# A convolution, layer norm and feed-forward kernel on one core: all 2,576 places of its order of operations replaced

## The chip, the core and the metric

The kernel runs on one core of a Trainium2 chip. The metric is the time of one execution on the device in microseconds (us). The median of several executions is compared; a separate execution is profiled, and every duration below comes from it.

A core has five engines, each with a queue of its own that it works off strictly in order: PE (TensorE: matrix products; PEld is its weight load), DVE (VectorE), ACT (ScalarE), POOL (GpSimd) and SP (SyncE, which here issues transfers and computes nothing). Transfers ("DMA") run beside the engines. An engine goes past an instruction only when what that instruction waits for has happened, so everything behind a waiting instruction on the same engine waits too.

## The reference

```python
# x (8, 4224, 192), weight_gen (8, 4224, 8 heads, 7 taps)
w = softmax(weight_gen, axis=-1)
y[b, s, h, :] = sum(w[b, s, h, k] * x_padded[b, s + k, h, :] for k in range(7))   # 24 wide a head
xn = (y - mean(y)) / sqrt(var(y) + 1e-6) * g_ln
out = y + relu(xn @ w_ch1) @ w_ch2          # 192 -> 768 -> 192
```

## The kernel before

The 33,792 tokens lie as 128 partitions x 264 columns, and the work goes by **groups** of four columns: group 0, 4, 8, ... 260, 66 in all (group 108 is columns 108 to 111). A group passes five steps.

1. SP loads x (`load`) and the taps (`wload`). DVE, POOL and ACT make the softmax, for twelve columns at a time (`max`, `sub`, `exp`, `sum`, `rcp`, `inv`, `mul`).
2. The convolution: DVE multiplies x by the taps in four instructions a group (`c0` to `c3` on line 527, three of them 1,536 wide into buffers `pr`, one 768 wide into `y`). Two of the six partial sums are added by accumulating transfers that POOL issues (`d0`, `d1`, line 533), four by POOL itself (`a0` to `a3`, line 530). The first four chunks go another way, over PE (`z`, line 548).
3. The layer norm: ACT makes the sums and the scaled rows (`sums`, `squares`, `rstd`, `xh` on line 631, `hi` on line 651), DVE five small steps (`newton`), POOL the low half of a split into two 16-bit halves (`lo`, line 664). SP turns the group by a transposing transfer (`turn`, line 668) into `xT`. There are two buffers `xh`, three `xT`.
4. The first product on PE: three `unit`s of 36 matmuls a group (line 686), each into one of two PSUM buffers `ph`. ACT evicts a unit with a relu (`relu`, line 701, into `hh`), DVE what its rounding left (`hlo`, line 703). Both must be done before PE may write that `ph` again, two units later.
5. The second product: two halves of 72 matmuls (`p0` and `p1`, line 737), for the group before the one whose units they stand among. Between them stands an empty instruction on SP (`hop`, line 747): `p0` must have ended before `hop`, and `hop` before `p1`. It costs nothing itself, but it stands in SP's queue behind transfers. DVE adds the result to `y` (`f`, line 789) and SP stores it (`u`, line 797).

Program order is made by a planner that records every operation with the engine that it runs on and what it needs. The order is not worked out in the kernel: `PLACE` gives each of the 2,576 operations a number, by kind and in the order in which that kind is recorded, and `order()` sorts by it. Each engine's queue is that sorted list cut down to its own operations. Where a pool has several buffers, the one whose last user has the lowest place is taken, so places also choose buffers.

Transposes and accumulating transfers are kept apart: a `turn` waits for the landing of the last `d0` or `d1` placed ahead of it, and the other way round.

```python
    def order(self):
        out = sorted(self.ops, key=lambda o: o.place)
...
                    b.slot = min(range(len(tenant[b.pool])), key=lambda i: freed(tenant[b.pool][i]))
...
            if o.kind in last:
                o.behind, last[o.kind] = last["turn" if o.kind == "add" else "add"], o
```

Of the kernel before, what the change touches and what calls it, by code (L numbers as in the profile page):

```python
# [32 lines left out]
        'wload': (1, 4, 28, 42, 57, 90, 73, 168, 448, 452, 507, 743, 618, 896, 787, 1151, 1181, 1307, 1553,  # L33
        1634, 1517, 1896, 1902),
        'load': (5, 14, 17, 32, 35, 75, 83, 109, 188, 121, 76, 182, 260, 236, 273, 363, 303, 497, 513, 390,
# [3 lines left out]
        'w_load': (39, 56, 53, 43, 44, 69),  # L39
        'w_load2': (115, 142),  # L40
        'w_as': (58, 61),
        'w_av': (62, 64, 71),
        'w_an': (92,),
        'w_cs': (66, 70),
        'w_cv': (77, 78, 81),
        'w_cn': (93,),
        'w_s1': (97, 98, 104, 108, 122),
        'w_h': (123, 135, 140, 146),
        'w_l': (153, 151),
        'w_m': (172, 180, 169, 165),  # L50
        'w_c2s': (124, 129, 155, 157),
        'w_c2v': (130, 133, 138, 158, 160, 161),
        'w_c2n': (152, 173),
        'w_s2': (177, 181, 184, 186, 198, 200, 211, 220),
        'max': (2, 7, 31, 55, 67, 117, 134, 258, 522, 464, 698, 858, 652, 1083, 1148, 1337, 1399, 1499, 1568,
        1730, 1612, 1962, 1996),
        'sub': (3, 8, 46, 72, 120, 250, 359, 439, 536, 672, 755, 987, 884, 1110, 1205, 1358, 1452, 1565, 1649,
        1766, 1943, 2020, 2100),
        'exp': (6, 12, 47, 84, 126, 256, 377, 465, 568, 750, 788, 996, 893, 1160, 1294, 1361, 1518, 1650,
        1653, 1831, 1994, 2099, 2112),  # L60
        'sum': (9, 15, 48, 99, 131, 268, 398, 469, 573, 771, 792, 998, 1049, 1172, 1299, 1365, 1519, 1679,
        1669, 1854, 2007, 2140, 2131),
        'rcp': (10, 24, 50, 102, 208, 342, 423, 524, 667, 807, 928, 1022, 1147, 1204, 1312, 1371, 1611, 1693,
        1677, 1919, 2027, 2164, 2205),
        'inv': (11, 26, 54, 118, 235, 356, 445, 528, 668, 859, 946, 1023, 1168, 1267, 1386, 1486, 1641, 1694,
        1792, 1961, 2072, 2189, 2238),
        'mul': (13, 30, 59, 189, 298, 399, 521, 637, 745, 863, 965, 1085, 1193, 1304, 1416, 1520, 1642, 1744,
        1870, 1983, 2086, 2190, 2343),
        'keep': (18, 34),
# [20 lines left out]
        'copy': (60, 74, 110, 167),  # L90
        'sums': (68, 82, 127, 125, 178, 174, 215, 213, 249, 253, 280, 275, 314, 323, 349, 351, 394, 434, 418,
# [7 lines left out]
        'squares': (80, 85, 147, 136, 190, 179, 226, 241, 271, 262, 291, 282, 338, 337, 355, 354, 395, 435,  # L99
# [7 lines left out]
        'rstd': (86, 149, 191, 242, 294, 361, 436, 511, 598, 671, 738, 815, 878, 959, 1036, 1111, 1186, 1248,  # L107
        1325, 1424, 1485, 1555, 1624, 1732, 1793, 1866, 1938, 2014, 2084, 2168, 2227, 2304, 2385, 2437, 2500),
        'newton': (87, 150, 194, 243, 297, 362, 437, 512, 599, 673, 740, 816, 880, 969, 1047, 1114, 1195,
# [912 lines left out]
```

## Time and profile before

| | us |
|---|---|
| median of 3 runs | 868.94 |
| lowest and highest | 864.72, 872.02 |
| profiled execution, its own time | 867.45 |
| its span, first to last instruction | 865.4 |
| PE busy in the span | 826.8 |
| DVE busy in the span | 771.2 |

The profiled execution took 1.49 us less than the median. Its span is 2.05 us shorter than its own time. Busy times of one engine are unions: two instructions that overlap count once. A matmul is shown longer than the distance to the next, because they are pipelined.

### The profile page before, as it was taken

What the parts mean: (1) busy time and instruction counts of PE and PEld (TensorE: products, weight loads), DVE (VectorE), ACT (ScalarE), POOL (GpSimd) and SP (SyncE); (2) the same over time, 40 slices, a digit from 0 to 9 for tenths busy, and PEclk for the clock granted to TensorE, in tenths of its full rate; (3) what the DMA queues carried; (4) which work ended last, traced back from release to release, by engine and by line L of the source; (5) the groups of instructions that cost most, each with busy time, mean ns of one, the idle gap of its engine ahead of it and who ended that gap; (6) DMA issues with size and microseconds to landing.
All of it is one profiled execution on the core that took longest, in us unless ns stands there. A gap on an engine that the chain in (4) does not pass through costs nothing.

```text
span 865.4 us, 37738 instructions
## 1 busy us (share of the span) xinstructions
PE 826.8 (96%) x16691; PEld 799.8 (92%) x16691; DVE 771.2 (89%) x863; ACT 683.5 (79%) x1797; POOL 728.9 (84%) x489
## 2 busy tenths in 40 slices
PE   5968999999999999999999899999999999999998
PEld 5547999999999999998999899999999999999987
DVE  6999999999999999999999799999999998775433
ACT  3888888978898798898789787979788888679721
POOL 6999899999999998999989888999999888777100
PEclk9979999999999999999999999999999999999999
DMA  8687778899969988879969776887886766644253
GB/s 223 157 203 148 156 150 169 179 190 202 194 149 188 198 187 185 164 143 216 198 137 176 194 169 143 190 170 182 175 186 148 155 152 148 120 103 92 68 112 93
DMA packets 146411, 140.91 MB, mean 163 GB/s; under 512 B 108487, under 2 KB 110415, under 8 KB 146247
## 3 DMA queue, kind: packets, MB, share of 16 engines
q1 hardware_dynamic: 127799, 88.95, 43.9%
q0 software_dynamic: 18144, 49.55, 30.7%
q8 instruction: 130, 2.13, 1.0%
q14 instruction: 34, 0.28, 0.1%
q10 hardware_dynamic: 304, 0.00, 0.0%
HBM read 36.43 MB, written 25.95 MB: 72 GB/s over the span
## 4 chain that ended last, share of the span: by engine, by line
PE 36%; DVE 13%; ACT 4%; POOL 4%; issue 3%; SPq 1%; DMA 1%; DVEq 0%; POOLq 0%; ACTq 0%
PE ph L686 18%; PE po L737 17%; DVE pr L527 5%; DVE hlo L703 3%; POOL y L530 3%; DVE y L527 1%; ACT hh L701 1%; DVE y L789 1%; ACT junk L585 1%; PE ph L766 1%; ACT xh L631 1%; DMA pr<-pr 1%; POOL hl L664 1%; ACT junk L580 1%; SPq L668 0%
## 5 line engine op out<-in xcount | busy, mean ns | idle before, releaser
L530 POOL TENSOR_TENSOR y<-y,pr 128x768 f32<-128x768 f32 x252 | 499.9, 2063 | 22.3 <-DVE pr L527 9.4
L686 PE MATMUL ph<-xT,c_w 64*128 64x256 f16 x7128 | 419.5, 272 | 9.0 <-DVE hlo L703 6.2
L686 PEld LDWEIGHTS <-c_w 64*128 64x128 f16 x7128 | 380.5, 95 | 23.1 <-issue 9.7
L737 PE MATMUL po<-c_w2h,hh 64*128 64x192 f16 x3120 | 387.2, 243 | 4.3 <-SPq L747 3.9
L737 PE MATMUL po<-c_w2l,hh 64*128 64x192 f16 x3120 | 387.1, 243 | 2.4 <-issue 2.4
L737 PE MATMUL po<-c_w2h,hlo 64*128 64x192 f16 x3120 | 387.1, 243 | 0.0
L527 DVE TENSOR_TENSOR pr<-x,wn 128x1536 f32<-128x1536 f32 (+1 forms) x193 | 332.2, 1736 | 2.8 <-DMA x<-in_x_dram 1.6
L737 PEld LDWEIGHTS <-hh 64*128 64x128 f16 x6240 | 303.7, 94 | 8.9 <-SPq L747 5.1
L703 DVE SCALAR_TENSOR_TENSOR hlo<-ph,hh 128x1024 f16<-128x1024 f32 x198 | 239.5, 1217 | 57.1 <-ACT hh L701 56.6
L701 ACT ACTIVATE hh<-ph 128x1024 f16<-128x1024 f32 x198 | 199.7, 1012 | 104.5 <-PE ph L686 103.8
L737 PEld LDWEIGHTS <-hlo 64*128 64x128 f16 x3120 | 172.2, 94 | 0.0
L664 POOL TENSOR_TENSOR hl<-xh,hl 128x768 f16<-128x768 f32 x66 | 123.2, 1931 | 36.2 <-ACT hl L651 36.2
L533 POOL DMA_DIRECT2D pr<-pr x126 | 123.6, 1135 | 27.3 <-DVE pr L527 14.9
L631 ACT ACTIVATE xh<-y,s 128x192 f32<-128x192 f32 x264 | 124.6, 535 | 16.9 <-DVE s L619 14.5
L585 ACT ACTIVATE junk<-y,s 128x192 f32<-128x192 f32 x264 | 119.5, 453 | 6.7
L580 ACT ACTIVATE junk<-y 128x192 f32<-128x192 f32 x264 | 94.8, 359 | 15.4 <-POOL y L530 9.8
L789 DVE SCALAR_TENSOR_TENSOR y<-po,c_fs,y 128x768 f32<-128x768 f32 (+1 forms) x66 | 65.8, 997 | 7.2 <-PE po L737 7.1
L527 DVE TENSOR_TENSOR y<-x,wn 128x768 f32<-128x768 f32 (+1 forms) x67 | 62.1, 933 | 1.1 <-ACT e L487 1.0
L651 ACT ACTIVATE hl<-xh 128x768 f16<-128x768 f32 x66 | 55.0, 837 | 1.0
L580 ACT ACTIVATION_READ_ACCUMULATOR junk<-y 128x1 f32 x264 | 49.6, 188 | 0.0
L585 ACT ACTIVATION_READ_ACCUMULATOR junk<-y,s 128x1 f32 x264 | 49.4, 187 | 0.0
L548 PE MATMUL ph<-pr,ident 128*128 128x192 f32 (+1 forms) x96 | 27.8, 447 | 12.4 <-DVE pr L527 10.4
(75 smaller groups left out, 324.4 us busy)
## 6 DMA issues: line engine op xcount, KB each, us to landing
pr<-pr POOLq DMA_DIRECT2D x126, 384.0 KB, 5.6
x<-in_x_dram SPq DMA_DIRECT2D x65, 384.0 KB, 5.5
out_dram<-y SPq DMA_DIRECT2D x64, 384.0 KB, 4.2
w<-in_weight_gen_dram SPq DMA_DIRECT2D x21, 336.0 KB, 5.6
pr<-in_moe_w_ch_dram SPq DMA_DIRECT2D x2, 576.0 KB, 5.6
xT<-hl SPq DMA_TRANSPOSE x66, 3.4
hh<-in_moe_w_ch_dram SPq DMA_DIRECT2D x1, 768.0 KB, 10.3
out_dram<-y SPq DMA_DIRECT2D x4, 192.0 KB, 2.6
```

Source lines behind the costliest of these rows:

```text
L527: E.tensor_tensor(out=ov, in0=xv, in1=wv, op=ALU.mult)
L530: Q.tensor_tensor(out=flat(0), in0=flat(0), in1=flat(k), op=ALU.add)
L533: return Q.dma_start(flat(to), flat(k), accum_op=ALU.add, max_dma_last_dim=CHUNK * D * 4)
L580: A.activation(junk, at(y)[:, j, :], AF.Identity, scale=-1.0 / D, accum_out=at(s4)[:, 3, t : t + 1])
L585: A.activation(junk, at(y)[:, j, :], AF.Square, bias=at(s4)[:, 3, t : t + 1], accum_out=at(s4)[:, 0, t : t + 1])
L631: A.activation(paired(xh, t), at(y)[:, i, :].rearrange("p (c q) -> p c q", q=P // 2), AF.Identity, bias=at(s4)[:, 3, g + t : g + t + 1], s ...
L664: lambda xh=xh, hl=hl: Q.tensor_tensor(out=halves(hl, True), in0=pairs(xh), in1=halves(hl, False), op=ALU.subtract),
L686: T_.matmul(ph[:, r, v * 2 * P : (v + 1) * 2 * P], W["w1"][rows, WB[r][c], w, f : f + P], xv[rows, a, c, :, :], start=(v == 0 and k == 0), ...
L701: lambda: A.activation(at(hh)[:, us, :], at(ph), AF.Relu), [ph], [(hh, u)])
L703: lambda: V.scalar_tensor_tensor(out=at(hlo)[:, us, :], in0=at(ph), scalar=0.0, in1=at(hh)[:, us, :], op0=ALU.max, op1=ALU.subtract),
L737: made.append(T_.matmul(at(po)[:, z, e * D : (e + 1) * D], token(b, 2 * z + e, j)[rows], W[w][rows, j, :], start=(ph == 0 and e == 0 and k ...
L789: V.scalar_tensor_tensor(out=ysl, in0=at(po)[:, zs[0] : zs[-1] + 1, : 2 * D], scalar=W["fs"][:, 0:1], in1=ysl, op0=ALU.mult, op1=ALU.add)
```

## The change

`PLACE` is the one thing that changes: every list in it has new numbers. The operations, their buffers' sizes and counts and all other code stay. The author's words for it: the same operations and buffers; all 2,576 places come from a new search whose replays hold late instruction blocks and long transfer issues.

PE's own order keeps 346 of 351 operations where they were; the five others are convolution sums in the first 16 operations. Of the others, 552 of 669 DVE operations, 688 of 775 of ACT, 397 of 482 of POOL and 236 of 299 of SP stand at another number of their queue, by 2 to 4 positions on the mean and 37 at most.

The last lines of the lists of `turn` and of `hop` (the last numbers are those of the last groups: for `turn` 252, 256, 260; for `hop` 248, 252, 256, 260):

```diff
-        'turn': (148, 195, 251, 285, 336, 370, 411, 432, 489, 505, 554, 581, 631, 654, 718, 727, 797, 804,
...
-        2137, 2181, 2223, 2254, 2285, 2298, 2353, 2330, 2405, 2448, 2476, 2507, 2517, 2520),
...
-        'hop': (240, 286, 324, 372, 405, 460, 493, 515, 559, 596, 626, 664, 719, 762, 801, 829, 871, 894, 949,
...
-        2278, 2301, 2324, 2359, 2391, 2426, 2461, 2484, 2515, 2531, 2546, 2560),
...
+        'turn': (157, 197, 255, 290, 336, 364, 404, 415, 494, 522, 557, 583, 633, 664, 721, 732, 788, 802,
...
+        2151, 2140, 2216, 2253, 2285, 2300, 2363, 2392, 2429, 2444, 2486, 2510, 2511, 2537),
...
+        'hop': (261, 291, 333, 380, 403, 444, 474, 528, 566, 602, 639, 679, 722, 753, 794, 840, 877, 919, 952,
...
+        2260, 2309, 2342, 2370, 2414, 2455, 2473, 2497, 2514, 2527, 2546, 2564),
```

In the rows of the order below a number behind a name is the buffer's. An empty instruction such as `hop` has no row.

**POOL while the pipeline fills, up to the low half of group 8** (L664 into hl_89; L533 are accumulating transfers, L530 adds, L458 the `sub` of a softmax, L953 a step of the weights). Before:

```order
39 L533 DMA pr_84<-pr_84 128x768
40 L533 DMA pr_82<-pr_82 128x768
41 L533 DMA pr_86<-pr_86 128x768
42 L533 DMA pr_81<-pr_81 128x768
43 L530 TENSOR_TENSOR y_73<-y_73,pr_80 128x768
44 L530 TENSOR_TENSOR y_72<-y_72,pr_84 128x768
45 L953 TENSOR_TENSOR c_w2l<-hlo_97,c_w2h 128x1152
46 L533 DMA pr_85<-pr_85 128x768
47 L533 DMA pr_83<-pr_83 128x768
48 L530 TENSOR_TENSOR y_72<-y_72,pr_86 128x768
49 L664 TENSOR_TENSOR hl_89<-xh_87,hl_89 128x2x384
50 L458 TENSOR_TENSOR e_104<-w_64,mx_99 128x672
```

After:

```order
39 L533 DMA pr_84<-pr_84 128x768
40 L530 TENSOR_TENSOR y_73<-y_73,pr_80 128x768
41 L533 DMA pr_81<-pr_81 128x768
42 L533 DMA pr_86<-pr_86 128x768
43 L533 DMA pr_85<-pr_85 128x768
44 L533 DMA pr_83<-pr_83 128x768
45 L533 DMA pr_82<-pr_82 128x768
46 L530 TENSOR_TENSOR y_72<-y_72,pr_84 128x768
47 L953 TENSOR_TENSOR c_w2l<-hlo_97,c_w2h 128x1152
48 L458 TENSOR_TENSOR e_104<-w_66,mx_99 128x672
49 L530 TENSOR_TENSOR y_72<-y_72,pr_86 128x768
50 L664 TENSOR_TENSOR hl_89<-xh_87,hl_89 128x2x384
```

Six transfers that stood as four and two stand as one and five, and one `sub` more stands ahead of the low half. On SP, not shown, `turn` of group 8 has moved from behind `hop` of group 4 (places 251 and 240) to ahead of it (255 and 261).

**ACT around the relu of the first unit of group 216** (L701, the row into hh_94 from ph_111 behind L631 or L430; L631 scales rows of groups 224 and 228 into xh, L585 and L580 are sums). Before:

```order
717 L701 ACTIVATE hh_95<-ph_112 128x1024
718 L580 ACTIVATE junk_109,s_107<-y_68 128x192 x2
719 L585 ACTIVATE junk_109,s_107<-y_68,s_107 128x192 x2
720 L631 ACTIVATE xh_87<-y_67,s_106 128x3x64 x2
721 L631 ACTIVATE xh_88<-y_75,s_106 128x3x64 x4
722 L701 ACTIVATE hh_94<-ph_111 128x1024
723 L631 ACTIVATE xh_87<-y_67,s_106 128x3x64 x2
```

After:

```order
714 L701 ACTIVATE hh_95<-ph_112 128x1024
715 L585 ACTIVATE junk_109,s_106<-y_71,s_106 128x192 x4
716 L608 ACTIVATE s_106<-s_106,bias 128x8
717 L609 ACTIVATE s_106<-s_106 128x8
718 L610 ACTIVATE s_106<-s_106 128x8
719 L430 COPY x<-x 128x1152
720 L701 ACTIVATE hh_94<-ph_111 128x1024
721 L631 ACTIVATE xh_88<-y_71,s_106 128x3x64 x2
722 L631 ACTIVATE xh_87<-y_74,s_106 128x3x64 x4
```

The scaled rows, which need a free buffer `xh`, have moved from ahead of the relu to behind it.

**SP near the end** (L668 are `turn`s, the last three those of groups 252, 256 and 260; L797 are stores). Before:

```order
198 L668 DMA_TRANSPOSE xT_91<-hl_90 128x12x128
199 L797 DMA out_dram<-y_67 16x8x768
200 L668 DMA_TRANSPOSE xT_93<-hl_89 128x12x128
201 L797 DMA out_dram<-y_68 16x8x768
202 L668 DMA_TRANSPOSE xT_92<-hl_90 128x12x128
203 L797 DMA out_dram<-y_70 16x8x768
```

After:

```order
201 L668 DMA_TRANSPOSE xT_91<-hl_90 128x12x128
202 L668 DMA_TRANSPOSE xT_93<-hl_89 128x12x128
203 L797 DMA out_dram<-y_77 16x8x768
204 L797 DMA out_dram<-y_76 16x8x768
205 L668 DMA_TRANSPOSE xT_92<-hl_90 128x12x128
```

By the numbers in the diff, `hop` of group 252 stood behind all three turns (2531 against 2507, 2517 and 2520); now it stands behind two of them (2527 against 2510 and 2511) and ahead of that of group 260 (2537).

## Rows read from the trace of the kernel before

**Rows 1.** The page's part 1: busy us (share of the span), instructions.

```profile
PE 826.8 (96%) x16691; PEld 799.8 (92%) x16691; DVE 771.2 (89%) x863; ACT 683.5 (79%) x1797; POOL 728.9 (84%) x489
```

**Rows 2.** Busy time by stage: PE, PEld, DVE, ACT, POOL; granted clock, DMA share, GB/s.

```profile
0.00:53.90 53.90, 35.24 (x131) 24.96 (x131) 45.16 (x75) 33.50 (x90) 45.64 (x34) 0.92 0.78 197
53.90:95.10 41.20, 34.74 (x615) 30.28 (x616) 39.20 (x52) 36.10 (x102) 40.20 (x30) 0.90 0.72 153
95.00:385.00 290.00, 288.91 (x6113) 285.06 (x6110) 285.07 (x307) 251.05 (x672) 275.49 (x185) 1.00 0.85 178
```

**Rows 3.** Groups by line: count | busy us, mean ns of one | idle before, releasers.

```profile
L686 PE MATMUL ph<-xT,c_w 64*128 64x256 f16 x7128 | 419.5, 272 | 9.0 <-DVE hlo L703 6.2 <-DMA xT<-hl 1.9
L527 DVE TENSOR_TENSOR pr<-x,wn 128x1536 f32<-128x1536 f32 x191 | 330.3, 1745 | 1.2
L703 DVE SCALAR_TENSOR_TENSOR hlo<-ph,hh 128x1024 f16<-128x1024 f32 x198 | 239.5, 1217 | 57.1 <-ACT hh L701 56.6
```

**Rows 4.** PE's waits from 95 us on: total, times, longest.

```profile
PE po L737 <- SPq L747: 3.9, 3, 1.6
PE po L737 <- issue: 2.4, 1, 2.4
PE ph L686 <- DVE hlo L703: 1.9, 3, 1.3
```

**Rows 5.** DVE's waits from 95 to 385 us, the longest of three rows.

```profile
DVE hlo L703 <- ACT hh L701: 0.5, 2, 0.3
```

**Rows 6.** Timeline of POOL: first of the six adds, group 8's low half, the next two.

```profile
59.58 0.87 POOL L533 DMA_DIRECT2D pr<-pr  x1
...
72.39 1.80 POOL L664 TENSOR_TENSOR hl<-xh,hl 128x768 f16<-128x768 f32 x1
74.00 1.51 POOL L458 TENSOR_TENSOR e<-w,mx 128x672 f32<-128x672 f32 x1
75.32 1.94 POOL L530 TENSOR_TENSOR y<-y,pr 128x768 f32<-128x768 f32 x1
```

**Rows 7.** SP and PE then: first hop (of 65), group 8's turn, its units.

```profile
L747 SPq EVENT_SEMAPHORE  x65: 17/17/17, 76.4 to 850.2; - x65
...
76.59 1.40 SPq L668 DMA_TRANSPOSE xT<-hl  x1
...
81.58 5.77 PE L686 MATMUL ph<-xT,c_w 64*128 64x256 f16 x72 [1.94 <-DMA xT<-hl]
```

**Rows 8.** ACT, DVE and PE around the first unit of group 216.

```profile
713.99 1.86 ACT L631 ACTIVATE xh<-y,s 128x192 f32<-128x192 f32 x4 [2.27 <-POOL hl L664]
715.76 1.00 ACT L701 ACTIVATE hh<-ph 128x1024 f16<-128x1024 f32 x1
...
716.79 1.22 DVE L703 SCALAR_TENSOR_TENSOR hlo<-ph,hh 128x1024 f16<-128x1024 f32 x1 [1.79 <-ACT hh L701]
...
718.07 0.48 PE L686 MATMUL ph<-xT,c_w 64*128 64x256 f16 x5 [1.35 <-DVE hlo L703]
```

**Rows 9.** SP and PE at the hop of group 252.

```profile
824.75 2.81 SPq L668 DMA_TRANSPOSE xT<-hl  x1
827.61 0.59 SPq L797 DMA_DIRECT2D out_dram<-y  x1
...
828.31 0.26 PE L737 MATMUL po<-c_w2h,hh 64*128 64x192 f16 x2 [1.58 <-SPq L747]
```

**Rows 10.** SP's turn ahead of the hop of group 108.

```profile
389.20 2.26 SPq L668 DMA_TRANSPOSE xT<-hl  x1
```

**Rows 11.** PE at 481 us, and the busy times and clock from 480 to 485.

```profile
481.43 0.26 PE L737 MATMUL po<-c_w2l,hh 64*128 64x192 f16 x2 [2.43 <-issue]
...
480.00:485.00 5.00, 3.57 (x42) 3.22 (x43) 3.31 (x4) 2.96 (x9) 4.84 (x4) 0.71 0.35 67
```

**Rows 12.** The page's part 3: queue of the accumulating transfers, and that of instructions.

```profile
q0 software_dynamic: 18144, 49.55, 30.7%
q8 instruction: 130, 2.13, 1.0%
```

More of the change, by code (lines that the diff above doesn't have):

```diff
@@ L32 @@
 PLACE = {
-        'wload': (1, 4, 28, 42, 57, 90, 73, 168, 448, 452, 507, 743, 618, 896, 787, 1151, 1181, 1307, 1553,
-        1634, 1517, 1896, 1902),
-        'load': (5, 14, 17, 32, 35, 75, 83, 109, 188, 121, 76, 182, 260, 236, 273, 363, 303, 497, 513, 390,
[3 rows of a table removed]
[L39 to L69, printed above, removed]
[20 rows of a table removed]
-        'copy': (60, 74, 110, 167),
-        'sums': (68, 82, 127, 125, 178, 174, 215, 213, 249, 253, 280, 275, 314, 323, 349, 351, 394, 434, 418,
[7 rows of a table removed]
-        'squares': (80, 85, 147, 136, 190, 179, 226, 241, 271, 262, 291, 282, 338, 337, 355, 354, 395, 435,
[7 rows of a table removed]
-        'rstd': (86, 149, 191, 242, 294, 361, 436, 511, 598, 671, 738, 815, 878, 959, 1036, 1111, 1186, 1248,
@@ L108 @@
-        1325, 1424, 1485, 1555, 1624, 1732, 1793, 1866, 1938, 2014, 2084, 2168, 2227, 2304, 2385, 2437, 2500),
-        'newton': (87, 150, 194, 243, 297, 362, 437, 512, 599, 673, 740, 816, 880, 969, 1047, 1114, 1195,
[14 rows of a table removed]
-        'wake': (154,),
[4 rows of a table removed]
-        'turn': (148, 195, 251, 285, 336, 370, 411, 432, 489, 505, 554, 581, 631, 654, 718, 727, 797, 804,
[27 rows of a table removed]
-        'halo': (305, 609, 819, 1281, 1507, 1821, 2260),
-        'unit': (185, 205, 209, 210, 230, 232, 252, 254, 283, 288, 316, 332, 339, 340, 365, 379, 386, 406,
[11 rows of a table removed]
@@ L170 @@
-        'relu': (192, 206, 218, 223, 237, 244, 272, 277, 299, 311, 319, 334, 360, 352, 366, 389, 400, 413,
[11 rows of a table removed]
-        'hlo': (199, 207, 219, 225, 239, 245, 276, 279, 301, 312, 320, 335, 364, 353, 368, 393, 402, 417, 429,
[15 rows of a table removed]
-        'hop': (240, 286, 324, 372, 405, 460, 493, 515, 559, 596, 626, 664, 719, 762, 801, 829, 871, 894, 949,
[16 rows of a table removed]
+        'wload': (1, 3, 13, 53, 58, 90, 134, 181, 433, 245, 591, 716, 712, 836, 945, 1207, 1208, 1371, 1422,
+        1592, 1528, 1959, 1883),
+        'load': (4, 6, 10, 25, 37, 78, 81, 104, 193, 188, 113, 236, 276, 222, 337, 348, 301, 501, 429, 399,
[3 rows of a table added]
@@ new lines @@
+        'w_load': (41, 48, 44, 55, 60, 2),
+        'w_load2': (94, 150),
+        'w_as': (56, 64),
+        'w_av': (68, 70, 72),
+        'w_an': (93,),
+        'w_cs': (63, 65),
+        'w_cv': (73, 82, 88),
+        'w_cn': (95,),
+        'w_s1': (96, 98, 103, 106, 117),
+        'w_h': (124, 137, 118, 123),
+        'w_l': (152, 125),
+        'w_m': (184, 187, 149, 141),
+        'w_c2s': (108, 111, 160, 161),
+        'w_c2v': (115, 127, 129, 162, 163, 166),
+        'w_c2n': (139, 175),
@@ new lines @@
+        'w_s2': (176, 179, 186, 196, 203, 208, 213, 227),
+        'max': (5, 8, 39, 69, 71, 107, 140, 232, 510, 407, 608, 845, 713, 940, 988, 1225, 1272, 1524, 1660,
+        1751, 1537, 2047, 1932),
+        'sub': (7, 9, 43, 74, 110, 229, 311, 437, 555, 658, 797, 976, 886, 1120, 1227, 1383, 1482, 1533, 1684,
+        1789, 1873, 2054, 2098),
+        'exp': (11, 17, 47, 91, 130, 249, 349, 476, 559, 670, 828, 982, 897, 1121, 1230, 1418, 1520, 1602,
+        1739, 1827, 1940, 2116, 2105),
+        'sum': (12, 19, 49, 105, 136, 250, 391, 480, 617, 676, 852, 987, 899, 1129, 1295, 1446, 1558, 1611,
@@ new lines @@
+        1744, 1854, 1969, 2146, 2106),
+        'rcp': (14, 20, 57, 114, 159, 322, 405, 489, 634, 730, 909, 1057, 1083, 1202, 1325, 1464, 1620, 1685,
+        1753, 1877, 2033, 2198, 2141),
+        'inv': (15, 34, 59, 128, 205, 323, 413, 516, 673, 771, 936, 1063, 1136, 1250, 1361, 1511, 1632, 1704,
+        1788, 1955, 2076, 2203, 2247),
+        'mul': (16, 36, 61, 189, 297, 390, 513, 627, 741, 849, 961, 1077, 1183, 1291, 1409, 1525, 1636, 1756,
+        1865, 1967, 2077, 2207, 2305),
+        'keep': (18, 40),
[20 rows of a table added]
@@ new lines @@
+        'copy': (62, 76, 131, 154),
+        'sums': (67, 84, 133, 132, 174, 177, 209, 185, 269, 266, 282, 278, 361, 330, 350, 347, 416, 420, 419,
[7 rows of a table added]
+        'squares': (83, 85, 143, 142, 180, 178, 220, 234, 273, 267, 283, 293, 362, 340, 372, 359, 438, 442,
[7 rows of a table added]
+        'rstd': (86, 147, 182, 235, 295, 374, 446, 515, 586, 665, 731, 808, 869, 964, 1046, 1118, 1175, 1265,
+        1332, 1393, 1484, 1548, 1625, 1715, 1779, 1861, 1939, 2005, 2090, 2159, 2248, 2311, 2377, 2425, 2484),
+        'newton': (89, 148, 183, 238, 296, 375, 447, 517, 587, 666, 743, 816, 870, 966, 1047, 1127, 1182,
[14 rows of a table added]
@@ new lines @@
+        'wake': (156,),
[4 rows of a table added]
+        'turn': (157, 197, 255, 290, 336, 364, 404, 415, 494, 522, 557, 583, 633, 664, 721, 732, 788, 802,
[27 rows of a table added]
+        'halo': (256, 595, 880, 1298, 1609, 1810, 2256),
+        'unit': (190, 194, 214, 216, 225, 242, 268, 277, 292, 307, 309, 324, 346, 355, 373, 386, 395, 406,
[11 rows of a table added]
+        'relu': (195, 211, 219, 228, 240, 243, 275, 280, 299, 313, 316, 332, 352, 356, 376, 388, 396, 409,
[11 rows of a table added]
+        'hlo': (200, 212, 224, 230, 247, 248, 279, 285, 300, 314, 320, 335, 353, 357, 379, 389, 397, 412, 427,
[15 rows of a table added]
```

266 rows, old and new, of the table PLACE are left out of this document.

## Prediction

> **What bounds the kernel now.** The page's busy times come first: PE is busy 96% of the span and DVE 89% [rows 1]. The instructions are the same afterwards, so only idle time and time at a lower clock can go. The span of 865.4 less PE's 826.8 leaves 38.6 us idle, and 53.90 - 35.24 = 18.7 of it lies ahead of the first unit at 53.9 us [rows 2], where PE waits for convolution, norm and weights to be made.
>
> Next the other stages [rows 2]. From 53.9 to 95.1 us PE is busy 34.7 of 41.2, with DVE (39.2) and POOL (40.2) nearly full: while the pipeline fills, those two set the pace. From 95 to 385 us PE is busy 288.9 of 290 and DVE 285.1 of 290, and DVE's longest row of waits there is 0.5 us in all [rows 5]. A busy share cannot tell which of two full engines leads; the waits can. DVE waits for nobody, so DVE's program order carries this stage as much as PE does: what is placed ahead of an hlo delays it by its whole length, unless PE was late anyway. From there on the idle time sits in single events. PE's list from 95 us [rows 4] holds 3.9 us in three waits for SP's hop, 2.4 in one wait that the profile gives to nothing but issue, and 1.9 for hlo.
>
> **The change part by part.** The sum is made against the profiled execution's own 867.45 us, which was 1.49 below the median of the three runs; I add that at the end. Ahead of the first unit DVE has the same 60 operations before the first hlo in both orders, and the weights' last step stands after the same DVE work, so I put the start at nothing. Its cover is DVE, full from 10 us on; one more or less wait there is worth about 1 us either way.
>
> (a) *Filling, group 8.* Its low half ends at 74.2 us, but the turn starts only at 76.59, straight behind the first hop at 76.4, and PE then waits 1.94 us and does the next two units in 5.77 us [rows 6, 7]. In the new order that turn stands ahead of that hop. One sub more stands ahead of the low half: 75.32 - 74.00 = 1.32 us [rows 6], so it ends at about 75.5, the turn starts at 75.6 instead of 76.6, and PE gets its rows 1.0 us earlier. The hop now has the turn's 1.40 us [rows 7] ahead of it and comes at 77.0 instead of 76.4; that moves the half behind it by 0.6 and cuts PE's wait to 1.94 - 1.0 - 0.6, about 0.4 us. The two units after the wait took 5.77 us against 2 x 36 x 419.5 / 7128 = 4.2 on average [rows 3], 1.5 us that I take to be the lower clock after the idle time. I count -1.0 - 1.5 = -2.5; the ends are 0 (the landing of the adds takes the place of the hop) and -1.94 - 1.5 = -3.4.
>
> (b) *DVE's lead.* I counted the DVE instructions ahead of each of the 198 hlo in both orders. The new one has more convolution in front: for example c1 twice, a c3 and a newton more and one inv less ahead of the hlo of the second unit of group 132 (4.9 us by the rows' means), 0.8 us more at group 164, nothing at group 8; on the mean over all hlo 1.9 us, about one 1,536-wide product of 1.745 us [rows 3]. Where DVE never waits [rows 5], this is paid: +1.9, with the ends 0 (PE is late anyway, as it is after any stall) and +2.4 (the point where the order's longest DVE path grows by most). It buys later conv results that lie ready, which helps (c) to (e).
>
> (c) *Group 216.* ACT sat 2.27 us before scaled rows that had no free xh until POOL had done an earlier low half; the relu behind them ended at 716.76, hlo at 718.01, and PE waited 1.35 us [rows 8]. The new order has this relu ahead of those rows. -1.35, ends 0 and -1.5 (with the slower first matmuls after it).
>
> (d) *Group 252.* SP issued a turn for 2.81 us and a store for 0.59 before the hop could pass, and PE waited 1.58 us [rows 9]. The turn of group 260 now stands behind that hop. -1.58, ends 0 and -1.8. What is late next there is that turn itself: it then starts right after the hop, and its group's first unit comes 6 blocks of PE later, so the cover is some 15 us.
>
> (e) *The other two hop waits*, 3.9 - 1.58 = 2.3 us: at group 108 the hop stood behind a turn that took 2.26 us to issue, against 1.40 for group 8's [rows 4, 7, 10]. In the new order that hop again has two turns straight ahead of it, and in each order 21 of 65 hops stand straight behind a turn. I count 0, with the ends -2.3 and +2.3.
>
> (f) *The late block of instructions.* [...] PE's own order is the same, so it asks for the same blocks. 0, with the ends -3.9 (none is late) and +3.9 (two are).
>
> [...]
>
> Sum: 867.45 - 2.5 + 1.9 - 1.35 - 1.58 = 863.9; with the 1.49 to the median, 865.4.
>
> **The rivals.** *Nothing late is left.* The block comes on time and no hop waits: (e) and (f) at their lower ends, 865.4 - 2.3 - 3.9 = 859.2. For it: more work lies ready, and hops and relus were taken out from behind two risky neighbours. Against it: blocks come by a queue on engines that PE's order does not govern, and as many hops stand behind turns. One execution with one such stall in some 130 blocks [rows 11, 12] speaks neither way. [...]
>
> *The order does not do what it says.* Each stall of the old order was one late event meeting a tight place; a new list has tight places of its own. (c) and (d) come back elsewhere, and (a) and (b) cancel but for 0.6: 867.45 - 2.5 + 1.9 + 1.49 = 868.3. For it: the counts under (e) are the same, and DVE's and POOL's queues have grown a little in front of what PE waits for.
>
> *Slower: the adds hold the transposes while the pipeline fills.* Six accumulating transfers, five in a row, now stand ahead of group 8's turn, which waits for the last of them, where the two last of six stood apart before. Such a transfer takes 0.307 x 865.4 / 126 = 2.1 us of all sixteen DMA engines [rows 12], 12.7 us for six. Issued from 59.6 us on [rows 6], beside three loads, they land at about 74 to 76 by my estimate, and the turn is ready at 75.5. It decides at 76.6, where the old turn began. If the last lands at 79, the turn is 2.4 us later than it was, PE's wait grows by that and none of (a) comes: 0 + 2.4, another 1.5 at the low clock, (b) at +2.4, and (c) and (d) lost in the same way as adds bunch again: 867.45 + 2.4 + 1.5 + 2.4 + 1.49 = 875.2.
>
> **How the numbers follow.** Forecast (863 to 868): 0.43. Nothing late: 0.22. Back elsewhere: 0.24. Slower: 0.11. One per cent of the median is 8.7 us, about what a measurement of this kernel can tell from no change. Faster by over 1% (below 860.2) is most of the second case and an edge of the first: 0.22. Slower by over 1% (above 877.6) is the upper half of the last: 0.07. The rest, 0.71, is within. The range leaves out a tenth on each side: below 857.5 all terms would have to stand at their good ends at once; 873.5 cuts the slower case in two.
>
> **What the profile will show.** (a) Group 8's turn at about 75.6 us, PE's wait before its units under 1 us and those two units in about 4.2. (b) Still no waits on DVE from 95 to 385 us; PE's busy time there 1 to 2 us below 288.9. (c), (d) No wait of PE over 1 us near 713 or 828. (e) One to four waits on the hop, each under 2 us. (f) One wait by issue of 2 to 3 us with a lower clock behind it, anywhere. I am wrong if PE's idle time ahead of its first unit changes by over 3 us, if DVE begins to wait for ACT in the middle, or if the turns of the first groups wait for adds.

## The result, and the profile after

| | before | after |
|---|---|---|
| median us (range of 7 runs) | 868.94 (864.72 to 872.02) | 860.75 (858.62 to 862.39) |
| profiled execution, its span | 867.45, 865.4 | 859.48, 857.4 |
| granted clock over the span | 0.988 | 0.995 |

The ratio is 0.9904, 95% interval 0.9879 to 0.9930: faster by 1%. The time lies in the predicted range (857.5 to 873.5), 4.7 us below the forecast of 865.4 and near the rival "nothing late is left" (859.2).

Part 1 of the page after. DVE does the same work in 1.6 us less, PE in 3.6 less [rows 1]:

```profile
PE 823.2 (96%) x16691; PEld 804.8 (94%) x16691; DVE 769.6 (90%) x863; ACT 685.4 (80%) x1797; POOL 728.6 (85%) x489
```

The stages after (columns as in [rows 2]: PE, PEld, DVE, ACT, POOL, clock, DMA share, GB/s):

```profile
53.10:95.10 42.00, 36.31 (x684) 32.97 (x686) 41.00 (x54) 37.38 (x100) 41.84 (x30) 0.95 0.76 162
95.00:385.00 290.00, 286.65 (x6050) 283.24 (x6046) 285.20 (x307) 247.66 (x658) 276.65 (x185) 1.00 0.87 179
385.00:640.00 255.00, 254.48 (x5398) 253.13 (x5396) 250.03 (x270) 218.77 (x584) 236.71 (x159) 1.00 0.87 180
```

The last of these stages in the kernel before:

```profile
385.00:640.00 255.00, 249.90 (x5270) 243.82 (x5268) 244.17 (x261) 208.45 (x551) 231.74 (x156) 0.99 0.83 177
```

From 95 to 385 us PE is busy 2.3 us less than in [rows 2] and DVE the same. From 385 to 640 DVE gets 5.9 us more work done in the same 255 us, PE 4.6: that is where most of the change lies in these two traces, and of the sum only (e), (f) and a part of (b) stood there. The rows of waits that the prediction took DVE's lead from end at 385 us [rows 5]; behind that DVE did wait, as the rows below show. In the changed kernel PE has nothing left to lose in this stage (254.48 of 255).

PE's waits from 95 us on, after (total, times, longest). The rows for SP's hop and for issue of [rows 4] are gone; what is left are short waits for DVE:

```profile
PE ph L686 <- DVE hlo L703: 3.5, 7, 1.1
PE po L737 <- DVE y L789: 1.6, 5, 0.5
```

DVE's waits from 385 to 640 us, first three rows of before, 6.9 us together:

```profile
DVE hlo L703 <- ACT hh L701: 4.2, 5, 2.3
DVE y L789 <- PE po L737: 1.7, 1, 1.7
DVE wn L615 <- ACT s L610: 1.0, 2, 0.5
```

and the only row of after:

```profile
DVE hlo L703 <- ACT hh L701: 1.3, 2, 0.8
```

Where the way from start to end got shorter shows best at the hlo of the first unit of group 168. Everything that DVE does up to it is nearly the same in both orders, so its start is DVE's busy time plus DVE's idle time. First before, with the window up to that start, then after:

```profile
571.63 1.22 DVE L703 SCALAR_TENSOR_TENSOR hlo<-ph,hh 128x1024 f16<-128x1024 f32 x1
...
0.00:571.60 571.60, 540.28 (x10655) 515.70 (x10657) 546.76 (x626) 471.38 (x1257) 530.47 (x358) 0.98 0.83 178
```

```profile
563.83 1.21 DVE L703 SCALAR_TENSOR_TENSOR hlo<-ph,hh 128x1024 f16<-128x1024 f32 x1
...
0.00:563.80 563.80, 535.70 (x10640) 518.62 (x10642) 546.50 (x626) 473.11 (x1258) 529.95 (x359) 0.99 0.86 179
```

626 instructions and 546.8 and 546.5 us of work; idle time 571.60 - 546.76 = 24.8 before, 17.3 after. The 7.5 us less are nearly the whole 8.0 of the span. Such a split can be made for any engine, so it does not show by itself that DVE sets the pace.

By the starts of PE's units the same two traces part like this (us; before_again is a second trace of the kernel before, group 12's start stands for its first unit, and so on):

| from, to | before | before_again | after | term of the sum |
|---|---|---|---|---|
| start, first unit | 53.9 | 53.9 | 53.1 | none |
| first unit, group 12 | 41.2 | 37.9 | 38.0 | (a) -2.5 |
| group 12, 96 | 250.9 | 254.1 | 254.2 | (b) +1.9 |
| group 96, 136 | 121.4 | 120.7 | 119.9 | (e) 0 |
| group 136, 148 | 40.0 | 39.5 | 35.5 | (f) 0 |
| group 148, 216 | 202.2 | 202.7 | 202.2 | none |
| group 216, 220 | 13.4 | 13.5 | 11.8 | (c) -1.35 |
| group 220, 228 | 23.7 | 23.7 | 25.6 | none |
| group 228, end | 118.8 | 118.6 | 117.0 | (d) -1.58 |

The largest single piece, 4.0 to 4.5 us, lies at the late block of instructions and the low clock behind it (0.71 from 480 to 485 us [rows 11]; 0.50 from 482.5 to 485 alone).

### The profile page after: what moved, and what is told of

It is laid out like the page before. It is cut to its first block, busy times and chain, and to the rows that moved or that the text cites. A ratio compares the mean times of both kernels' runs of the same rounds, so it can differ in the third digit from the quotient of the medians.

```text
span 857.4 us, 37760 instructions
## 1 busy us (share of the span) xinstructions
PE 823.2 (96%) x16691; PEld 804.8 (94%) x16691; DVE 769.6 (90%) x863; ACT 685.4 (80%) x1797; POOL 728.6 (85%) x489
## 4 chain that ended last, share of the span: by engine, by line
PE 53%; DVE 22%; POOL 9%; ACT 7%; issue 6%; DMA 2%; SPq 0%; DVEq 0%; POOLq 0%; ACTq 0%
PE ph L686 27%; PE po L737 26%; DVE pr L527 10%; POOL y L530 6%; DVE hlo L703 5%; DVE y L527 2%; ACT junk L585 2%; ACT hh L701 2%; POOL pr L533 1%; ACT junk L580 1%; POOL hl L664 1%; DVE y L789 1%; ACT xh L631 1%; DMA pr<-pr 1%; DMA x<-in_x_dram 1%
## 5 line engine op out<-in xcount | busy, mean ns | idle before, releaser
L530 POOL TENSOR_TENSOR y<-y,pr 128x768 f32<-128x768 f32 x252 | 500.0, 2074 | 20.7 <-DMA pr<-pr 9.4
L686 PEld LDWEIGHTS <-c_w 64*128 64x128 f16 x7128 | 385.2, 94 | 16.5 <-issue 12.6
L737 PEld LDWEIGHTS <-hh 64*128 64x128 f16 x6240 | 308.8, 94 | 3.2 <-issue 2.7
L703 DVE SCALAR_TENSOR_TENSOR hlo<-ph,hh 128x1024 f16<-128x1024 f32 x198 | 238.2, 1215 | 53.9 <-ACT hh L701 53.6
L701 ACT ACTIVATE hh<-ph 128x1024 f16<-128x1024 f32 x198 | 199.3, 1013 | 92.6 <-PE ph L686 85.7
L737 PEld LDWEIGHTS <-hlo 64*128 64x128 f16 x3120 | 176.8, 94 | 0.0
L664 POOL TENSOR_TENSOR hl<-xh,hl 128x768 f16<-128x768 f32 x66 | 124.1, 1929 | 38.5 <-ACT hl L651 38.3
L533 POOL DMA_DIRECT2D pr<-pr x126 | 125.2, 1218 | 18.6 <-DVE pr L527 6.1
L631 ACT ACTIVATE xh<-y,s 128x192 f32<-128x192 f32 x264 | 124.7, 535 | 17.1 <-DVE s L619 14.7
L585 ACT ACTIVATE junk<-y,s 128x192 f32<-128x192 f32 x264 | 119.7, 453 | 7.1
L580 ACT ACTIVATE junk<-y 128x192 f32<-128x192 f32 x264 | 95.0, 360 | 19.8 <-POOL y L530 13.5
L580 ACT ACTIVATION_READ_ACCUMULATOR junk<-y 128x1 f32 x264 | 49.5, 187 | 0.0
L585 ACT ACTIVATION_READ_ACCUMULATOR junk<-y,s 128x1 f32 x264 | 49.4, 187 | 0.0
L458 POOL TENSOR_TENSOR e<-w,mx 128x672 f32<-128x672 f32 (+2 forms) x23 | 36.0, 1565 | 2.8 <-DVE mx L456 2.7
```

Of the source, the lines that this page charges most:

```text
L530: Q.tensor_tensor(out=flat(0), in0=flat(0), in1=flat(k), op=ALU.add)
L533: return Q.dma_start(flat(to), flat(k), accum_op=ALU.add, max_dma_last_dim=CHUNK * D * 4)
L580: A.activation(junk, at(y)[:, j, :], AF.Identity, scale=-1.0 / D, accum_out=at(s4)[:, 3, t : t + 1])
L585: A.activation(junk, at(y)[:, j, :], AF.Square, bias=at(s4)[:, 3, t : t + 1], accum_out=at(s4)[:, 0, t : t + 1])
L631: A.activation(paired(xh, t), at(y)[:, i, :].rearrange("p (c q) -> p c q", q=P // 2), AF.Identity, bias=at(s4)[:, 3, g + t : g + t + 1], s ...
L664: lambda xh=xh, hl=hl: Q.tensor_tensor(out=halves(hl, True), in0=pairs(xh), in1=halves(hl, False), op=ALU.subtract),
```

## The experiments

The table holds all kernels, the two of the comparison included. "Unit 96" is the start of PE's first unit of group 96 in the profiled execution, "unit 168" that of group 168 ("96 to 168" in the text is the difference of the two), "rest" what is left of the span, "DVE idle" is the window's idle time up to the hlo of group 168, as above. (The expectations count it some 1.3 us lower, with small instructions that the windows don't call busy.) The ratio is to runs of the kernel before on the same chip (17 or 29; medians 866.2, 865.7 and 866.3 in the three sets); for after it is that of the first table. Each kernel has one profiled execution, so the columns from the first unit on are single readings.

| kernel | median us | ratio (95%) | first unit | unit 96 | unit 168 | rest | DVE idle |
|---|---|---|---|---|---|---|---|
| before | 868.94 | 1 | 53.9 | 346.0 | 566.9 | 298.5 | 24.8 |
| before_again | 866.43 | one run | 53.9 | 345.9 | 565.6 | 298.9 | 23.7 |
| fill_new | 862.94 | 0.9964 (0.9948 to 0.9981) | 52.6 | 343.2 | 561.0 | 298.8 | 19.3 |
| fill_old | 864.17 | 0.9981 (0.9954 to 1.0008) | 54.6 | 349.9 | 564.7 | 297.3 | 21.0 |
| local | 864.23 | 0.9985 (0.9967 to 1.0004) | 53.7 | 346.3 | 566.1 | 296.2 | 24.1 |
| spread | 865.74 | 0.9991 (0.9971 to 1.0011) | 54.3 | 344.4 | 562.8 | 301.5 | 21.0 |
| best1 | 859.76 | 0.9924 (0.9903 to 0.9946) | 53.4 | 344.0 | 562.1 | 295.8 | 20.5 |
| after | 860.75 | 0.9904 (0.9879 to 0.9930) | 53.1 | 345.4 | 560.1 | 297.3 | 17.3 |
| after_again | 859.92 | 0.9933 (0.9911 to 0.9955) | 52.5 | 345.7 | 560.4 | 297.3 | 17.5 |
| after_pair | 859.73 | 0.9925 (0.9898 to 0.9953) | 53.2 | 345.3 | 560.0 | 298.3 | 17.2 |
| early | 872.32 | 1.0070 (1.0051 to 1.0089) | 53.4 | 351.0 | 571.8 | 298.3 | 28.0 |
| late_before | 872.78 | 1.0080 (1.0048 to 1.0111) | 53.9 | 350.2 | 572.2 | 298.0 | 28.0 |
| late_after | 865.32 | 0.9987 (0.9969 to 1.0006) | 52.9 | 347.3 | 565.6 | 298.3 | 21.5 |
| best2 | 857.79 | 0.9900 (0.9869 to 0.9930) | 55.2 | 347.0 | 562.0 | 295.4 | 19.0 |

The first four share one set of theories: single late events that add up (1), the lead of convolution, that is, how much of it stands ahead of an hlo in DVE's queue (2), a mere shift in time (3).

**A second look at the kernel before** (no edit).

> The kernel before, unchanged, for a second look. If the late events are tied to the order (theory 1), the three hop waits of 1.0 to 1.6 us, the wait at group 216 and PE's stall of 2.4 us by issue at 481 us stand at the same places to within some tenths. If the stall is a matter of when the instruction queue's transfers meet others in this execution, it is gone, shorter, or at another of PE's block boundaries, while the hop waits stay.

```profile
PE po L737 <- SPq L747: 3.8, 5, 1.5
PE ph L686 <- DVE hlo L703: 2.6, 5, 1.4
PE po L737 <- issue: 2.1, 2, 1.9
```

The late events belong to the order: the stall by issue stands at the same instruction (480.09 us, 1.93 long), the waits at groups 116, 216 and 252 are there with 0.95, 1.44 and 1.45 us. The wait at group 108 fell under 0.5, and group 8's wait of 1.94 [rows 7] is gone, though the turn came at 76.58 as before; the kernel still reached group 96 at 345.9 against 346.0. So 3.3 us of PE's lost time in the filling (groups 4 to 11) made no difference 250 us later.

**The new filling with the old rest, and the reverse.** One list of the filling and the start of one that runs through, fill_new against before:

```diff
-        'w_load': (39, 56, 53, 43, 44, 69),
+        'w_load': (41, 48, 44, 55, 60, 2),
...
-        'u': (292, 563, 367, 374, 514, 724, 485, 519, 780, 640, 615, 889, 966, 778, 1165, 922, 866, 1014, 956,
+        'u': (312, 563, 368, 375, 514, 724, 485, 519, 780, 640, 615, 889, 966, 778, 1165, 922, 866, 1014, 956,
```

> The new order up to the point where the pipeline is full (its first 310 places, about 95 us), the old order behind it. Theory 1 (single late events): the two traces lose 3.9 us less in the new filling (0.8 before the first unit, 3.1 from there to group 12), and everything behind is the old order with its late hops, relu and block, so this kernel comes at about 865.0 us against 868.9 for the kernel before. Theory 2 (the gain is the lead of convolution that the new order builds and keeps in the middle): the old order behind the filling sets the time, 868 to 869. Theory 3 (a shift in time alone makes the old order's late events miss their tight places): 861 to 863, with the hop waits and the late block of the kernel before gone although their order is the old one.

> The old order for the first 310 places, the new one behind it. Theory 1: the new order behind the filling has no late hop, no late relu at group 216 and, in its one trace, no late block, and pays small waits for hlo: 4.1 us less, about 864.8 us; group 8's wait of some 1.9 us and its two slow units come back. Theory 2: nearly all of the gain is here, 861 to 862. Theory 3: 866 to 868, with new late events of 1 to 2.5 us in other places, since the new order meets the old order's times.

The new filling gives 3.3 us at the median, the new rest 2.0 (its interval reaches to nothing); together 5.3, where the changed kernel's two further runs had 5.8 and 6.5 on these chips. So the change is not in one place. fill_new reaches group 96 2.8 us sooner than before, and DVE has been idle 2.3 us less by the hlo of that group's second unit: 356.10 - 340.78 = 15.3 before (first row), 13.0 in fill_new.

```profile
0.00:356.10 356.10, 329.91 (x6242) 311.53 (x6244) 340.78 (x400) 294.49 (x788) 333.57 (x228) 0.98 0.83 179
```

```profile
0.00:353.30 353.30, 327.53 (x6243) 307.97 (x6245) 340.26 (x400) 295.01 (x788) 333.87 (x228) 0.99 0.83 181
```

These are two single traces: 1.3 of the 2.8 us lie ahead of the first unit, and spread below, whose order is the old one far beyond that point, is at group 96 at 344.4. fill_new is there also 2.2 us sooner than the changed kernel, which has the same filling and more lead (best1, with fill_new's order up to there, 1.4): that is what the lead seems to cost up to there, though all engines' orders differ between the two. From 96 to 168 the changed kernel takes 214.7 us and fill_new 217.8, its late block among it: the price comes back. The five traces with the new order's hlo there all take 214.7 to 215.0 (fill_old too), those with the old order 217.8 or more. fill_old shows the order meeting strange times: PE waits 2.05 us at 109 us for a transpose. Theory 3 fails: fill_new keeps the late block (1.75 us) and two hop waits of 3.4 us in all.

**Five local moves in the old order.** Two of them, the relu of group 216 on ACT and the turn of group 116 on SP:

```diff
+L701 ACTIVATE hh0_94<-ph0_111 128x1024
 L631 ACTIVATE xh1_88<-y8_75,s40_106 128x3x64 x4
-L701 ACTIVATE hh0_94<-ph0_111 128x1024
...
-L668 DMA_TRANSPOSE xT2_93<-hl1_90 128x12x128
 L797 DMA out_0_dram<-y9_76 16x8x768
+L668 DMA_TRANSPOSE xT2_93<-hl1_90 128x12x128
```

> The kernel before with five local moves and nothing else: group 8's turn ahead of the first hop, the relu of group 216 ahead of the scaled rows, and three turns (groups 116, 124 and 260, the latter two with one load and one store) behind the hops of groups 116, 108 and 252 that they held up. Theory 1: each wait goes and nothing comes for it: 2.5 to 3.1 for group 8, 1.35, 1.6 and 2.3 for the others, some 7.8 us in all, about 861 us; the lead of convolution is the old one, so nothing is paid for it, and only the late block may stay. Theory 2: what is late next takes their place within a group or two, 866 to 868. Theory 3: between them, about 864, with new waits of over 1 us elsewhere.

PE's waits from 95 us on: the hop is gone from the list, hlo has grown from 1.9 to 4.4.

```profile
PE ph L686 <- DVE hlo L703: 4.4, 10, 1.3
PE po L737 <- issue: 2.2, 1, 2.2
PE po L737 <- DVE y L789: 0.5, 2, 0.3
```

The median is 2.0 us lower instead of 7.8 (the interval reaches to nothing), in the trace all of it in the rest (298.5 or 298.9 to 296.2), where (c) and (d) went and nothing came for them. Ahead of it the moves brought nothing: 346.3 and 219.8 against 345.9 and 219.7 in before_again. Group 8's move put a longer wait in the place of the old one. The turn had no hop ahead of it now, but it waited for the accumulating transfers ahead of it, the last of which landed at 77.65; it came at 77.70, the hop behind it, and the half waited. In the kernel before, the last of them had landed at 75.58, so the hop had held this turn for 0.9 us at most. First SP's wait from 70 to 79 us, then the rows:

```profile
SPq L668 <- DMA pr<-pr: 21.5, 1, 21.5
...
77.70 1.40 SPq L668 DMA_TRANSPOSE xT<-hl  x1
...
79.21 0.26 PE L737 MATMUL po<-c_w2h,hh 64*128 64x192 f16 x2 [2.81 <-SPq L747]
```

Theory 1 in its plain form falls: such events add up only in the rest. Theory 3's forecast for this kernel fits (about 864, with new waits of over 1 us: PE waits 1.27 and 1.11 us for hlo at groups 116 and 120), though fill_new speaks against it. I put in its place, as theory 1 of the next set, that DVE paces up to group 168 and PE behind it; its theory 2 there is luck.

**The late block's cause.** Two accumulating transfers on POOL go later in the kernel before:

```diff
-L533 DMA pr5_85<-pr5_85 128x768
-L533 DMA pr3_83<-pr3_83 128x768
-L533 DMA pr6_86<-pr6_86 128x768
+L533 DMA pr3_83<-pr3_83 128x768
...
+L533 DMA pr5_85<-pr5_85 128x768
...
+L533 DMA pr6_86<-pr6_86 128x768
```

> The kernel before with two accumulating transfers of POOL moved and nothing else: those of group 164, which stood with one of group 160 in three within 1.1 us, go 3.5 and 10 us later. If it is this burst that holds PE's next instruction block (it began 11.3 us behind the one before it, where 6 is usual), the stall of 1.9 to 2.4 us in the half of group 136 is gone and the block begins at most 8 us behind the one before. What that is worth: 3.9 us if PE paces there (the stall and its low clock, 862 to 863 where the kernel before takes 866.5); 2 to 3 us if DVE paces and only its waits for the late half count. If the block hangs on the weights' load or on PE's own order, the stall stays and the time is that of the kernel before.

In the kernel before, POOL issues four such transfers in one go at 465.41 us (first row). From 468.6 to 478.4 us the DMA list has no row for the queue of instructions (a block is here one packet of it [rows 12]), and the accumulating queue takes 80.7% of the engines:

```profile
465.41 3.54 POOL L533 DMA_DIRECT2D pr<-pr  x4 [0.27 <-issue]
...
q0 software_dynamic: 514, 1.38, 80.7%
q1 hardware_dynamic: 275, 0.72, 23.6%
```

The block behind began 11.3 us after the one before it (467.17 and 478.50). With the two transfers moved it began 6.0 after (465.32 and 471.33), PE had no stall, and its clock, 0.71 in [rows 11], was full:

```profile
480.00:485.00 5.00, 5.00 (x115) 5.00 (x112) 5.00 (x5) 4.22 (x10) 4.92 (x4) 1.00 0.68 161
```

All five traces with the old order of POOL there have the stall (before, before_again, local, fill_new, late_before: 2.43, 1.93, 2.18, 1.75, 2.09); the two with these transfers moved and the seven with the new order behind the filling don't have it there. The cause of this stall is shown. Such stalls are not gone from the new order for good: in late_after four such transfers go out between 511.75 and 517.08 us, the block behind begins 10.8 us after the one before (511.00 and 521.84), and PE stands 1.01 us at 524.12; early has one of 0.98 at 511.43. In the changed kernel four go out in the same way from 509.24 on, and the next block comes 6.2 us after the one before: such transfers do not always hold it.

Its worth is another matter. From group 136 to 148 spread takes 36.4 us against 39.5 and 40.0, so 3.1 to 3.6 of the 3.9 were there; by group 168 1.9 of them were lost again, with new waits of PE for DVE (1.4 us), and from 96 to 168 it takes 218.4 against 219.7 and 220.9. It starts group 168 at 562.8, 2.8 sooner than before_again (1.5 of that was there at group 96, ahead of the edit), and ends at the same time (spans of 864.3 and 864.5). 2.2 us were lost at group 216, where ACT waits for POOL, which had not become faster. Rows of spread that answer to [rows 8]; PE's wait there grew from 1.35 or 1.44 to 2.01, and the unit behind it took 2.97 instead of 2.14:

```profile
711.58 1.86 ACT L631 ACTIVATE xh<-y,s 128x192 f32<-128x192 f32 x4 [2.94 <-POOL hl L664]
713.35 1.00 ACT L701 ACTIVATE hh<-ph 128x1024 f16<-128x1024 f32 x1
...
715.66 2.97 PE L686 MATMUL ph<-xT,c_w 64*128 64x256 f16 x36 [2.01 <-DVE hlo L703]
```

**The parts together.** best1 is fill_new with the edit of spread and two of the moves of local, the relu of group 216 and the turn of group 260.

> The new order for the first 310 places, the old one behind it, with the two transfers spread and with the relu of group 216 and the turn of group 260 moved. Theory 1 (what pays is: the filling through DVE, the late block, and the last two waits, where PE paces): fill_new's span of 859.8 less 1.3, 1.5 and some 2 for the block: 855 of span, about 857 us, below the changed kernel. If gains here are lost again as the moves around groups 108 and 116 were: 860 to 862.

859.76 us: the level of the changed kernel, not the 857 expected. Against fill_new the rest is 3.0 us less, as with the local moves; from 96 to 168 the block is on time, but the time is 218.1 against 217.8, with two hop waits of 2.4 us. Once more the block's removal shows little behind it.

**The changed kernel again**, twice (no edit).

> The changed kernel, unchanged, beside the kernels below. Theory 1 (DVE is the pacer up to group 168, and the change pays through the idle time that DVE no longer has there): 0.990 of the kernel before, about 859 us where that one takes 867; no stall by issue in the half of group 136; DVE has been idle for about 16 us by the hlo of group 168, against 22 to 23.5 in the old order. Theory 2 (the middle was lucky in its one trace): a late block or a hop wait of over 1 us shows up in this second trace, and the time is 861 to 863.

> The changed kernel once more, beside the three others of this call: 858 to 861 us, with DVE idle for 16 us by the hlo of group 168.

859.92 and 859.73; no late block at group 136 in three traces, and only one hop wait (0.7 us, in the last).

**Less lead, more lead.** In early, 82 hlo of the changed kernel stand one product earlier; in late_before and late_after, 64 of the kernel before and 63 of the changed one stand one later. The first place of each, early against after and late_after against after:

```diff
+L703 SCALAR_TENSOR_TENSOR hlo1_97<-ph1_112,hh1_95 128x1024
 L527 TENSOR_TENSOR y10_77<-x_63,wn0_110 128x768
-L703 SCALAR_TENSOR_TENSOR hlo1_97<-ph1_112,hh1_95 128x1024
...
-L703 SCALAR_TENSOR_TENSOR hlo1_97<-ph1_112,hh1_95 128x1024
-L527 TENSOR_TENSOR pr0_80<-x_63,wn0_110 128x1536
+L527 TENSOR_TENSOR pr0_80<-x_63,wn0_110 128x1536
+L703 SCALAR_TENSOR_TENSOR hlo1_97<-ph1_112,hh1_95 128x1024
```

> The changed kernel with less lead: in 82 places between groups 12 and 168 an hlo changes places with the one convolution product that stands straight ahead of it on DVE (1.0 to 1.75 us). By the prediction's step (b), where the lead is a price of 1.9 us, this is 1 to 2 us faster than the changed kernel. By theory 1 the lead is a loan, paid back when the convolution ends, and the cushion from which DVE works while PE is late: DVE waits more for ACT's relu, its idle time by group 168 grows from 16 to 18 to 25 us, and the kernel is 2 to 8 us slower than the changed one.

> The kernel before with more lead: in 64 places between groups 12 and 168 one hlo goes behind the convolution product that stood straight behind it (0.84 us more convolution ahead of an hlo on the mean; the change itself adds 1.9). By the prediction's step (b), a price: 0.8 us or more slower. By theory 1 in its plain form (any lead is a cushion): DVE waits less for ACT, its idle time by group 168 falls from 22 to 23.5 to some 19, and the kernel is 2 to 4 us faster. A third reading, that what counts is not the mean lead but that each hlo stands where its relu is ready and PE does not yet need it: this one and the next are both slower, by 1 to 6 us, PE waiting for hlo.

> The changed kernel with the same shift, 63 hlo each one product later. Step (b): 0.8 us slower. Plain theory 1: 0 to 2 us faster, since only 2.5 us of DVE's waits for ACT are left to take away. Third reading: 2 to 8 us slower, PE's waits for hlo growing from 3.5 to 10 us or more.

All three are slower than the kernel they start from: 12.4, 6.5 and 5.6 us. The last lies in the range of the third reading (2 to 8); the first two lost more than expected (2 to 8 by theory 1, 1 to 6 by the third reading). With the hlo earlier, DVE stands at a relu that is not ready; its first row from 95 to 640 us:

```profile
DVE hlo L703 <- ACT hh L701: 10.9, 16, 1.7
```

With the hlo later, PE waits for it; first rows from 95 us on of late_before and of late_after (1.9 and 3.5 us in the kernels they start from):

```profile
PE ph L686 <- DVE hlo L703: 10.2, 16, 1.5
```

```profile
PE ph L686 <- DVE hlo L703: 8.9, 16, 1.2
```

Plain theory 1 (any lead is a cushion) falls with late_before, and (b), a price and nothing else, falls with early, which still has 0.83 us more lead than the kernel before (mean over the 118 hlo of groups 12 to 168, by DVE's durations in its trace). What fits all three is the third reading: an hlo has room between its relu's end and PE's need, and it is the fit to this room that is worth something.

**Two moves behind 640 us** in the changed kernel, where PE has its longest wait from 95 us on. ACT stood 5.08 us at a sum that waited for POOL, the relu behind it:

```profile
732.25 0.36 ACT L580 ACTIVATE junk<-y 128x192 f32<-128x192 f32 x1 [5.08 <-POOL y L530]
...
733.10 1.00 ACT L701 ACTIVATE hh<-ph 128x1024 f16<-128x1024 f32 x1
...
735.41 1.81 PE L686 MATMUL ph<-xT,c_w 64*128 64x256 f16 x30 [1.06 <-DVE hlo L703]
```

```diff
+L701 ACTIVATE hh0_94<-ph0_111 128x1024
 L580 ACTIVATE junk0_109,s42_108<-y1_68 128x192 x2
-L701 ACTIVATE hh0_94<-ph0_111 128x1024
...
-L527 TENSOR_TENSOR pr0_80<-x_63,wn0_110 128x1536
 L789 SCALAR_TENSOR_TENSOR y3_70<-po0_113,c_fs_132,y3_70 128x768
+L527 TENSOR_TENSOR pr0_80<-x_63,wn0_110 128x1536
```

> The changed kernel with two moves behind 640 us and nothing else: one relu of group 225 ahead of a scaled sum that waits for POOL, and the output step of group 220 ahead of a convolution product. If PE paces there (theory 1), both waits of PE (1.06 us near 735 and 0.46 near 731) go and nothing comes for them: 1.5 us less than the changed kernel beside it, about 0.2%. If some other engine paces there, the waits reappear within a few groups and the span is the same to within 0.3 us.

PE's list has no wait left behind 640 us, and the rest is 295.4 against 297.3, 297.3 and 298.3: 1.9 to 2.9 us less. The median is 857.79 against 859.73 for the changed kernel beside it (six runs each, 856.85 to 859.47 and 858.95 to 860.70). It is the fastest kernel here, ahead of the kernel before for certain and of the changed one probably. Its profiled execution reached the first unit 2 us late, at 55.2, which no edit explains.

## Why the prediction came out as it did

**The range held; the forecast was 4.7 us too slow.** It stood for a change of -3.5 us; the first comparison has -8.2, the two later ones -5.8 and -6.5, where the kernel before is some 3 us faster. The steps that failed are (e) and (f), both taken at 0, (b) as a price that stays, and the sum over PE's waits to which they belong. **(f)** argued that PE's own order asks for the same blocks, so one is late again: but the block was late (11.3 us behind the one before it, 6.0 in spread) because of the transfers that POOL had issued ahead of it, and these the order does govern. It came on time in three of three traces, and the 4.0 to 4.5 us between groups 136 and 148 are near the term's lower end, -3.9. No run shows that 3.9 as such: it was my estimate from [rows 11], 2.43 us of wait and (1 - 0.71) x 5 = 1.45 at the low clock; spread, with the block on time, took 3.1 to 3.6 less there. So the rival "nothing late is left" (0.22) is nearest to what came. **(e)** counted hops that stand straight behind a turn, and the count did not change; the waits did, from 3.9 us with that of (d) to nothing, nothing and 0.7.

**(a)** went further in the trace than it said: the turn at 73.93, earlier than the 75.6 forecast, the two units in 4.09 us without a wait and at a clock of 1.00, where the kernel before had 0.50 from 83 to 86 us, within these units. All six accumulating transfers had been issued by 63.80 us instead of 68.96; the last landed at 73.84, and the low half ended at 73.91:

```profile
73.93 1.42 SPq L668 DMA_TRANSPOSE xT<-hl  x1
...
79.35 4.09 PE L686 MATMUL ph<-xT,c_w 64*128 64x256 f16 x72
```

But it was not worth the 2.5 us: the same wait was absent in before_again at no gain, and in local the move made a longer one. What the new filling is worth, 2.8 us at group 96 in its trace, goes with DVE's 2.3 us less of idle time.

**(b)** had a size that fits up to group 96 (1.4 to 2.2 for the 1.9, if all of it is the lead's), which may be luck, and the wrong end of the story: it is a loan. DVE's work up to the end of the convolution is the same in both orders, so what was done early is not done later, and from group 96 to 168 the changed kernel gained 5.0 to 6.2 us on the kernel before (214.7 against 219.7 and 220.9).

**(c), (d)** went, and paid about in full, as local and best1 show in their rest (2.3 to 3.0 for the 2.9); in the changed kernel half of it or more was taken back by new waits at 731 and 735 us, which I had not looked for.

The deeper fault is the sum itself. I wrote that DVE's order carries the middle, and then added up PE's waits. Up to group 96 a PE wait showed no cost (346.0, 345.9 and 346.3 in three traces whose waits in the filling differ by over 3 us; spread, with the same order up to there and as little time lost as before_again, has 344.4). From there to 168 a wait taken away alone (local, spread) brought new ones for DVE and paid nothing or a part; in the changed kernel no such waits came, and it paid in full. Behind 640 us it counts in full. The rival "slower" did not happen: in the new filling the transfers landed as the low half ended. Its mechanism is there in local, where they hold group 8's turn until 77.65.

**Open.** Over 29 runs on one chip the kernel before ranged from 861.9 to 872.7, the changed one over 12 on two chips from 858.9 to 862.5. The kernels with the new filling spread over 1.5 to 3.8 us, those with the old one over 5 to 11. What in the old filling makes it so was not tried; from the first unit to group 12 the six traces with it take 37.9 to 41.2 us, the eight with the new one 38.0 to 38.1. Of the 5 to 6 us between groups 96 and 168, 0.8 to 1.6 lie ahead of group 136, with its two hops, and 4.0 to 4.5 at the late block. Taken away alone, the block gave 1.3 to 2.5 by group 168 and the hops nothing; that the changed kernel keeps all of it by the fit of its hlo is argued, not shown by a run that moves these alone.

## What to carry to other kernels

Ask of each stage which engine's idle time moves the end: take a point behind it, and split its time into that engine's busy and idle time up to there. In such a stage, mending one wait of another engine may only move the wait (in local PE's waits for the hop went and those for hlo grew from 1.9 to 4.4 us), while in a stage that this engine does not pace a local move pays at once (1.9 to 2.9 us in best2's rest). Where each engine works off a list in order, an instruction that is not ready holds up everything behind it (ACT stood 5.08 us at a sum, a relu behind it): look for the long idle time of a helper engine with a ready and wanted operation right behind it.

## What was not expected of the hardware

Accumulating transfers issued close together (four in one go from 465.41 us) held the transfer of PE's next instruction block: in the kernel before it began 11.3 us behind the one before it, in spread, with two of the transfers later, 6.0. In the five traces with the transfers in one go PE stood 1.75 to 2.43 us in the half of group 136 with all its data there, in spread not at all. In the changed kernel four such transfers from 509.24 us on did not hold the next block, which came 6.2 us after the one before.
